# Moving the weight-splitting work of a fused delta-rule attention and MLP kernel ahead of its layer products

## The chip, the cores and the metric

The kernel runs on one core of one Trainium2 chip. A core has a matrix engine (TensorE, PE in the profile, with its weight loads shown as PEld), VectorE (DVE), ScalarE (ACT), GpSimd (POOL) and SyncE (SP), which here only issues DMAs. The metric is the device time of one execution in microseconds (us), lower is better; it is 635.78 us in the median of three runs (633.97 to 636.45).

## The reference

A delta-rule attention over 768 tokens for 4 batches of 8 heads of width 48, then a two-layer MLP with a squared relu on the 3072 tokens.

```python
# attention: q, k, v (4, 8, 768, 48), beta (4, 8, 768), all float32
k_n = k / (norm(k) + 1e-06)
for t in range(S):
    y[:, :, t] = einsum('bhd,bhde->bhe', q[:, :, t], state)
    v_old = einsum('bhde,bhd->bhe', state, k_n[:, :, t])
    state = state + beta_t * einsum('bhd,bhe->bhde', k_n[:, :, t], v[:, :, t] - v_old)
# MLP: x is y as (3072, 384); w_in (384, 2048), w_out (2048, 384)
h = maximum(x @ w_in, 0.0)
return (h * h @ w_out).astype(float32)
```

## The kernel before

**Units.** The 768 tokens are cut into 12 units of 64 tokens (u = 0 to 11). For each unit the kernel loads keys, queries, values and beta, normalizes the keys (`normalize`: squares on ACT, L310; their sums on DVE, L314; root, reciprocals, the scaling of the keys, L326), transposes keys and queries on PE and copies them out on ACT (L363, L366), forms the products of keys with keys and with queries (L379), inverts a triangular matrix for each head on DVE (`invert`, L556 and L557, for units 2 and on, and `invert_both` for units 0 and 1), carries the state on (`state_part`: L609, L620, L646, L671, L689, L706), and puts the unit's 256 rows (64 tokens of 4 batches) through the MLP (`moe`). The inversion of unit 2 works on a matrix `lt` that is written to DRAM in blocks and read back by DMA.

**The MLP of one unit.** `moe` transposes the rows, splits them into a high part x_h (ACT, L729) and a low part x_l (DVE, L730), and runs 8 pairs of layer steps. A first step is 9 products into a bank h (L762: high weights with x_h, low weights with x_h, high weights with x_l, 3 chunks each). When both steps of a pair are done, ACT does relu, square and a cast (L771, L772, L774) and DVE the low half h_l (L739). Two pairs later come the second-layer steps, 6 products each (L747), into two banks o. The 36 layer products of the title are the first four of these first-layer steps; a unit has 16 first-layer steps (9 products) and 16 second-layer steps (6 products).

**The weights.** w_in and w_out come from DRAM as 28 parts (numbered 0 to 27 in the order of loading, `w0` to `w27` in the names: 3 of w_in, 4 of w_out, and so on). Each is split on the chip into a high and a low half before it can be used, once: a scaling on ACT (L142), then **W** words (three DVE instructions, L150, L152, L154), **H** the cast to the high half on ACT (L160), **R** the remainder on DVE (L174), **L** the low half: two PE products into a PSUM bank (L167, L168) and a copy out of it on ACT (L169). The parts 0 to 9 are split before the first MLP; the parts 10 to 27 are split while unit 0's MLP runs, in two stretches: a hand-written order after `take(chain, 1)` (L895 to L926), and then the weave of u = 1, which lays the steps of several generators at places between 0 and 1. In the weave the low halves are not listed: `settle` (L227) is called after the products of a layer step of unit 0 and does one if there is a remainder more than there is a cast in hand, `word` does some if more than two parts are under way, and `half` does what is missing when a product needs it.

**Order.** Within each engine the instructions run in the order in which the program writes them (`tc.manual_schedule`); engines wait for each other by semaphores. So an instruction that waits holds up all that stand behind it on its engine. The low halves use one two-bank tile g in pairs (the first of a pair needs both copies, L169, of the pair before), and single banks x where `spare` is off. All loads of the stretch go through SP's queue in order: queries of unit 2 (L270, which wait until PE has transposed the queries of unit 1, L363), w20, w21, beta of unit 2, values of unit 1, then what the inversion of units 0 and 1 sends (L530, L535, after DVE's L519), w22 to w27, keys of unit 3, and the blocks for `lt` (L397, L407).

Of the kernel before, what the change touches and what calls it, by code (L numbers as in the profile page):

```python
# [21 lines left out]
def kernel(  # L22
# [96 lines left out]
    FIRST = 7  # L119
# [16 lines left out]
    def split_weights():  # L136
# [8 lines left out]
        def words(x):  # L145
            raw = raws[x]
            w1 = raw[:, :, 1]
            a, rest = room(x, w1.shape[1])

            nc.vector.tensor_scalar(out=a, in0=w1, scalar1=3, scalar2=None, op0=ALU.logical_shift_left)  # L150

            nc.vector.tensor_scalar(out=w1, in0=w1, scalar1=3, scalar2=-0x800000, op0=ALU.logical_shift_left,  # L152
                                    op1=ALU.bitwise_and)
            nc.vector.scalar_tensor_tensor(out=rest.bitcast(F32R), in0=raw[:, :, 0].bitcast(U32), scalar=2.0 ** -52,  # L154
                                           in1=w1.bitcast(F32), op0=ALU.mult, op1=ALU.mult)
            return x, a, rest
# [38 lines left out]
        def word():  # L195
            while woven[0] and summed and len(formed + casted + summed) > 2:
                join()
            formed.append(words(*ready.pop(0)))

        def cast():  # L200
# [6 lines left out]

        def join():
            low(*summed.pop(0), formed=True)

        steps_of = dict(W=word, H=cast, R=remain, L=join)

# [14 lines left out]
        def settle():  # L227

            if hold[0] or not woven[0]:
                hold[0] = max(0, hold[0] - 1)  # L230
            elif len(summed) > (len(casted) > 0):
                work("L")

        def half(*key):
# [1 line left out]
                work("L" if summed else "R")  # L236
            return halves[key]

        casted, summed = [], []
        ready, formed, waiting, done = [], [], [], [0]  # L240
        return scaled, worded, highs, lows, work, late(), settle, half

# [474 lines left out]
    def moe(d):  # L717
# [23 lines left out]
        def second(fp):  # L741
            h_h, h_l = hs[fp]
            for e in range(2):
                ft = 2 * fp + e
                for i in range(2):
                    for n, (a, w) in enumerate(((h_h, 0), (h_h, 1), (h_l, 0))):
                        nc.tensor.matmul(o[i], lhsT=a[:, e, i * P:(i + 1) * P], rhs=half("wo", ft)[w],  # L747
                                         start=(ft == 0 and n == 0), stop=(ft == FT - 1 and n == 2))
                if d["u"] == 0:
                    settle()  # L750
                rest()
                yield

        for fp in range(FT // 2):
            hp = ps_h.tile([P, PC], F32, name="h").rearrange("p (e t) -> p e t", e=2)
            for e in range(2):
                ft = 2 * fp + e
                f = slice(ft % EACH * P, (ft % EACH + 1) * P)
                n = 0
                for w, x in ((0, x_h), (1, x_h), (0, x_l)):  # L760
                    for kt in range(KT):
                        nc.tensor.matmul(hp[:, e], lhsT=half("wi", (kt, ft // EACH))[w][:, f], rhs=x[:, kt],  # L762
                                         start=(n == 0), stop=(n == 3 * KT - 1))
                        n += 1
                if e == 0:
                    if d["u"] == 0:
                        settle()
                    rest()
                    yield
            r = mpool.tile([P, 2, 2 * P], F32, name="r")  # L770
            nc.scalar.activation(out=r, in_=hp, func=AF.Relu)  # L771
            nc.scalar.activation(out=r, in_=r, func=AF.Square)  # L772
            h_h = mpool.tile([P, 2, 2 * P], F32R, name="h_h", bufs=3)
            nc.scalar.copy(out=h_h, in_=r)  # L774
            h_l = mpool.tile([P, 2, 2 * P], F32R, name="h_l", bufs=3)
            later.append((r, h_h, h_l))
            hs.append((h_h, h_l))
            yield
            if fp > 1:
                yield from second(fp - 2)  # L780
# [13 lines left out]
    def take(gen, n=None):  # L794
        while n is None or n > 0:
            try:
                next(gen)
            except StopIteration:
                return
            if n is not None:  # L800
                n -= 1
# [19 lines left out]
    def bank_spared():  # L821
        del halves_free[:]
        spare[0] = True
        yield

    def late_loads():
        load_beta(ds_[2])
        load_v(ds_[1])
        yield
        fetch(NW)  # L830
        yield
# [21 lines left out]
    with tc.manual_schedule(engines=engines):  # L853
# [53 lines left out]
        first, third = moe(ds_[0]), normalize(ds_[2])  # L907
        take(first, 1)
        split_early = False
        spare[0] = True  # L910
        work("L")
        take(first, 2)
        work("HRHR")
        take(first, 2)
        work("LL")
        take(chain, 1)
        take(pair[1], 2)
        work("WHRL")
        take(first, 1)
        take(pair[1], 1)  # L920
        load_q(ds_[2])
        fetch(2)
        take(third, 1)
        work("W")
        take(third, 1)
        work("HRL")  # L926
        spare[0] = False
        used = FIRST + 10
        before = None
        woven[0] = True  # L930
        corner, inverse = inverse, None
        for u in range(1, units):
            parts = []
            begun = J0 if u == 1 else I0
            n_i = round((1 - begun) / (I1 - begun) * NI)
            if inverse:
                parts.append((inverse, left))
            getting, now = loads(u), moe(ds_[u - 1]) if u > 1 else first
            parts += [(now, [-2])] if u > 1 else []
            if u < units - 1:  # L940
                parts.append((static(ds_[u + 1]), [-1, 0.155, 0.165] if u > 1 else [0.14, 0.215, 0.225]))
            inverse = invert(ds_[u + 1]) if u < units - 1 else None
            if inverse:
                parts.append((inverse, steps(n_i, begun, 1)))
                left = steps(NI - n_i, 0, I1 - 1) + [0.16]
            if u == 1:
                parts.append((corner, [0.01, 0.035, 0.075, 0.115, 0.12, 0.13]))
                parts.append((third, [0.01, 0.015, 0.03, 0.045]))
                parts.append((late_loads(), [0.08, 0.131]))
                parts.append((bank_spared(), [0.1305]))  # L950
                parts.append((splits, steps(2 * (NW - used) + 1, 0, 0.7)))
                parts.append((pair[1], [0.25]))
            parts += [(getting, L1 + steps(6, *N1) if u > 1 else [0.135] + steps(6, 0.55, 0.9)),
                      (state_part(ds_[u]), [x / STEPS for x in (CHAIN if u > 1 else CHAIN1)])]
            if before:
                parts += [(before, [x / STEPS for x in range(OVER)] + [0.2, 0.21])]
            parts.append((now, [x / STEPS for x in range(OVER, STEPS)] if u > 1 else steps(STEPS - OVER - 5, 0, 1)))
            weave(*parts)
            before = now
        final = moe(ds_[units - 1])  # L960
# [33 lines left out]
```

## Time and profile before

| what | value |
|---|---|
| median of 3 runs | 635.78 us (633.97 to 636.45) |
| the profiled execution | 635.26 us, span 633.5 us from the first to the last instruction |
| PE busy in the span | 591.6 us (93%) |
| DVE, ACT, POOL busy | 418.2 us (66%), 317.7 us (50%), 29.8 us (5%) |
| mean granted clock of TensorE | 0.96 of full speed |
| DMA | 49.32 MB, 78 GB/s on average |

Busy time is a sum over instructions of an engine. A matmul's end is modelled, so busy PE time is not work at the peak rate: at the lower of the two clocks (1.2 GHz instead of 2.4 GHz, shown as 0.50) the same products are busy for longer. Idle time of an engine that nothing waits for costs nothing.

### The profile page before, as it was taken

To read this page: it belongs to the slowest core of one execution; us is meant where nothing else is said; L and a number is where in the kernel's file an instruction comes from. 1 tells how busy PE (TensorE), PEld (TensorE's weight loads), DVE (VectorE), ACT (ScalarE), POOL (GpSimd) and SP (SyncE) were. 2 spreads that over 40 slices of the span, in tenths; PEclk is the share of its full clock that TensorE was granted. 3 is DMA by queue.
4 is the path that set the end of the run, shared out by engine and by line. 5 is a ranking of instruction groups with operands and counts; after the bars stand their busy time and mean duration, and the time that the engine had idled before them with its cause. 6 is when DMAs were issued, how large, how long until landed. Compare 5 with 4: busy or idle time off the path is not lost.

```text
span 633.5 us, 23879 instructions
## 1 busy us (share of the span) xinstructions
PE 591.6 (93%) x10390; PEld 557.8 (88%) x10390; DVE 418.2 (66%) x1130; ACT 317.7 (50%) x623; POOL 29.8 (5%) x52
## 2 busy tenths in 40 slices
PE   2859787899999999999999999999999999999997
PEld 2547676789999999999999999999999999999997
DVE  4697357798686694795794785875876865941211
ACT  4736655745454545445435536455454535355442
POOL 4000000000101001001001001001010010000000
PEclk9955779899999999999999999999999999999999
DMA  7667347612624524427217217226235144030101
GB/s 213 159 172 186 94 100 209 103 31 40 111 53 64 86 50 85 75 39 117 55 27 125 55 32 122 57 40 112 53 49 98 27 65 82 2 68 2 26 1 26
DMA packets 172464, 49.32 MB, mean 78 GB/s; under 512 B 164288, under 2 KB 167368, under 8 KB 172360
## 3 DMA queue, kind: packets, MB, share of 16 engines
q1 hardware_dynamic: 168840, 47.06, 37.1%
q8 instruction: 82, 1.34, 0.9%
q10 hardware_dynamic: 3392, 0.72, 0.6%
q14 instruction: 22, 0.18, 0.1%
q0 software_dynamic: 128, 0.01, 0.0%
HBM read 36.54 MB, written 10.49 MB: 74 GB/s over the span
## 4 chain that ended last, share of the span: by engine, by line
PE 80%; ACT 2%; issue 0%; DVE 0%; ACTq 0%; DVEq 0%
PE o L747 32%; PE h L762 31%; PE g L646 2%; PE x L646 2%; PE x L671 2%; PE g L706 2%; PE x L379 1%; PE g L379 1%; PE x L689 1%; PE h L609 1%; PE x L620 1%; PE h L726 1%; PE x L363 1%; PE g L363 1%; ACT w L169 0%
## 5 line engine op out<-in xcount | busy, mean ns | idle before, releaser
L747 PE MATMUL o<-w,h_h 128*128 128x384 f32 x768 | 204.7, 348 | 0.0
L771 ACT ACTIVATE r<-h 128x512 f32<-128x512 f32 x96 | 57.5, 599 | 231.9 <-PE h L762 231.8
L762 PE MATMUL h<-x_h,w 128*128 128x256 f32 x1152 | 171.9, 285 | 0.4 <-DVE x_l L730 0.3
L739 DVE TENSOR_TENSOR h_l<-r,h_h 128x512 fp32r<-128x512 f32 x96 | 67.7, 705 | 139.3 <-ACT h_h L774 139.3
L762 PEld LDWEIGHTS h<-x_h,w 128*128 128x128 f32 x1152 | 156.4, 192 | 2.0 <-ACT x_h L729 0.8
L747 PEld LDWEIGHTS o<-w,h_h 128*128 128x128 f32 x768 | 134.5, 189 | 3.2
L747 PE MATMUL o<-w,h_l 128*128 128x384 f32 x384 | 130.4, 340 | 0.0
L556 DVE SCALAR_TENSOR_TENSOR tmp<-lt,bt,z 128x126 f32<-128x126 f32 (+22 forms) x310 | 95.7, 309 | 9.5 <-DMA lt<-blocks 1.7
L762 PE MATMUL h<-x_l,w 128*128 128x256 f32 x576 | 100.7, 284 | 0.0
L557 DVE TENSOR_TENSOR z<-z,tmp 128x126 f32<-128x126 f32 (+22 forms) x310 | 79.2, 256 | 10.6
L762 PEld LDWEIGHTS h<-x_l,w 128*128 128x128 f32 x576 | 82.8, 191 | 0.0
L747 PEld LDWEIGHTS o<-w,h_l 128*128 128x128 f32 x384 | 72.6, 189 | 0.0
L772 ACT ACTIVATE r<-r 128x512 f32<-128x512 f32 x96 | 60.7, 632 | 3.1
L774 ACT CAST h_h<-r 128x512 fp32r<-128x512 f32 x96 | 59.5, 620 | 3.1
L545 POOL MEMSET z<- 128x512 f32 x10 | 5.3, 527 | 454.8 <-DMA inv<-z 273.4
L697 DVE TENSOR_TENSOR state<-state,x 48x384 f32<-48x384 f32 x40 | 22.0, 550 | 0.8 <-PE x L689 0.3
L379 PE MATMUL x<-kq 48*64 48x64 f32 (+1 forms) x608 | 19.1, 255 | 0.7 <-ACT kq L366 0.7
L379 PEld LDWEIGHTS x<-kq 48*64 48x64 f32 x608 | 16.8, 152 | 2.8 <-ACT kq L366 1.1
L142 ACT ACTIVATE w<-w 128x384 f32<-128x384 f32 (+1 forms) x28 | 16.7, 613 | 4.6 <-DMA w<-in_moe_w_in_dram 4.6
L363 PE MATMUL x<-plus,kpad 64*128 64x64 f32 x96 | 6.5, 240 | 11.3 <-DVE kpad L326 11.3
L624 ACT ACTIVATE tt<-x 32x256 f32<-32x256 f32 x44 | 16.4, 373 | 0.5
L154 DVE SCALAR_TENSOR_TENSOR rest<-w 128x384 fp32r<-128x384 uint32 (+1 forms) x21 | 13.3, 634 | 4.5 <-PE g L168 2.4
(150 smaller groups left out, 627.9 us busy)
## 6 DMA issues: line engine op xcount, KB each, us to landing
w<-in_moe_w_in_dram SPq DMA_DIRECT2D x12, 512.0 KB
w<-in_moe_w_out_dram SPq DMA_DIRECT2D x16, 384.0 KB
lt<-blocks SPq DMA_DIRECT2D x20, 256.0 KB
qpad<-in_q_dram SPq DMA_DIRECT2D x96, 48.0 KB
vt<-in_v_dram SPq DMA_DIRECT2D x48, 96.0 KB
out_dram<-a SPq DMA_DIRECT2D x46, 96.0 KB
kpad<-in_k_dram SPq DMA_DIRECT2D x88, 48.0 KB
blocks<-ap SPq DMA_DIRECT2D x40, 64.0 KB
```

Of the source, the lines that this page charges most:

```text
L363: nc.tensor.transpose(pair[b][:, x, p], src[rows, c, 2 * p:2 * p + 2].rearrange("p a b -> p (a b)"), ident[rows, rows])
L379: nc.tensor.matmul(ps[j][to * C:(to + 1) * C, p, (x - first) * C:(x - first + m) * C], lhsT=kq[rows, c, p, b, 0], rhs=kq[rows, c, p, b, x: ...
L556: nc.vector.scalar_tensor_tensor(out=tmp, scalar=bt[:, s:s + 1], op0=ALU.mult, op1=ALU.mult, **factors)
L557: nc.vector.tensor_tensor(out=z[:, :nj, s + 1:], in0=z[:, :nj, s + 1:], in1=tmp, op=ALU.subtract)
L646: nc.tensor.matmul(dst[j][to, c, p], lhsT=d["kq"][rows, c, p, b, x], rhs=state[rows, b, c, p], start=(c == 0 and p == 0) if x else True, s ...
L697: nc.vector.tensor_tensor(out=state[rows, b], in0=state[rows, b], in1=ku[b][rows], op=ALU.add)
L739: nc.vector.tensor_tensor(out=h_l, in0=r, in1=h_h.bitcast(F32), op=ALU.subtract)
L747: nc.tensor.matmul(o[i], lhsT=a[:, e, i * P:(i + 1) * P], rhs=half("wo", ft)[w], start=(ft == 0 and n == 0), stop=(ft == FT - 1 and n == 2))
L762: nc.tensor.matmul(hp[:, e], lhsT=half("wi", (kt, ft // EACH))[w][:, f], rhs=x[:, kt], start=(n == 0), stop=(n == 3 * KT - 1))
L771: nc.scalar.activation(out=r, in_=hp, func=AF.Relu)
L772: nc.scalar.activation(out=r, in_=r, func=AF.Square)
L774: nc.scalar.copy(out=h_h, in_=r)
```

## The change

Unit 0's MLP and the splitting of parts 11 to 27 are written in another order. In the hand-written stretch the low halves and casts stand ahead of the first layer steps, and the squares of the third keys (unit 2) directly after the first relu. In `moe`, `settle` is called ahead of a layer step's products, where before it was called behind them, and it is called for the second step of a pair (in the first layer from the fourth pair on for both). `settle` has another condition (a counter `ripe`: a remainder that was made before the last `word`). In the weave of u = 1 the places of the inversion of units 0 and 1 (`corner`), of unit 2's transposes and of the late loads are moved back by 0.02 to 0.04, and the MLP has one step fewer left.

```diff
@@ split_weights
         def word():
             while woven[0] and summed and len(formed + casted + summed) > 2:
                 join()
+            ripe[0] = len(summed)
             formed.append(words(*ready.pop(0)))
 ...
         def join():
             low(*summed.pop(0), formed=True)
+            ripe[0] = max(0, ripe[0] - 1)
 ...
             if hold[0] or not woven[0]:
                 hold[0] = max(0, hold[0] - 1)
-            elif len(summed) > (len(casted) > 0):
+            elif ripe[0] or summed and not formed and not ready:
                 work("L")
@@ moe, second layer
                 ft = 2 * fp + e
+                if d["u"] == 0 and e:
+                    settle()
                 for i in range(2):
                     for n, (a, w) in enumerate(((h_h, 0), (h_h, 1), (h_l, 0))):
 ...
-                if d["u"] == 0:
-                    settle()
                 rest()
@@ moe, first layer
                 ft = 2 * fp + e
+                if d["u"] == 0 and (e or fp > 2):
+                    settle()
                 f = slice(ft % EACH * P, (ft % EACH + 1) * P)
 ...
                 if e == 0:
-                    if d["u"] == 0:
-                        settle()
                     rest()
@@ the hand-written stretch
-        spare[0] = True
-        work("L")
+        spare[0] = woven[0] = True
+        hold[0] = 0
+        work("LHRHRL")
         take(first, 2)
-        work("HRHR")
+        take(third, 1)
         take(first, 2)
-        work("LL")
+        take(third, 1)
         take(chain, 1)
+        work("W")
+        take(first, 1)
         take(pair[1], 2)
-        work("WHRL")
+        work("HR")
+        take(third, 1)
         take(first, 1)
         take(pair[1], 1)
         load_q(ds_[2])
         fetch(2)
-        take(third, 1)
-        work("W")
-        take(third, 1)
-        work("HRL")
         spare[0] = False
-        used = FIRST + 10
+        used = FIRST + 9
         before = None
-        woven[0] = True
@@ the weave of u = 1
-                parts.append((static(ds_[u + 1]), [-1, 0.155, 0.165] if u > 1 else [0.14, 0.215, 0.225]))
+                parts.append((static(ds_[u + 1]), [-1, 0.155, 0.165] if u > 1 else [0.18, 0.25, 0.26]))
 ...
-                parts.append((corner, [0.01, 0.035, 0.075, 0.115, 0.12, 0.13]))
-                parts.append((third, [0.01, 0.015, 0.03, 0.045]))
-                parts.append((late_loads(), [0.08, 0.131]))
+                parts.append((corner, [0.03, 0.075, 0.12, 0.16, 0.165, 0.17]))
+                parts.append((third, [0.005, 0.02, 0.03]))
+                parts.append((late_loads(), [0.08, 0.171]))
```

No instruction is added or removed on any engine; on POOL nothing moves, and SP's DMAs keep their order.

The first place is ACT, from the first relu of unit 0's MLP on (`h_960` and `h_971` are the first pair's bank, `kpad2` the third keys, `g_954` the bank with the low halves of parts 10 and 11). Before:

```order
L771 ACTIVATE r_979<-h_960 128x512
L772 ACTIVATE r_979<-r_979 128x512
L774 CAST h_h_982<-r_979 128x512
L160 CAST w13_985<-r_886 128x384
L142 ACTIVATE w15_705<-w15_705 128x512
L142 ACTIVATE w16_707<-w16_707 128x512
L160 CAST w14_990<-a_892 128x512
L771 ACTIVATE r_1013<-h_993 128x512
L772 ACTIVATE r_1013<-r_1013 128x512
L774 CAST h_h_1016<-r_1013 128x512
L169 CAST w11_833<-g_954 128x384
L169 CAST w12_883<-g_1022 128x384
```

And in the changed program, whose lines from the relu on are two higher:

```order
L160 CAST w13_958<-r_886 128x384
L142 ACTIVATE w15_705<-w15_705 128x512
L142 ACTIVATE w16_707<-w16_707 128x512
L160 CAST w14_963<-a_892 128x512
L169 CAST w11_833<-g_954 128x384
L773 ACTIVATE r_990<-h_971 128x512
L774 ACTIVATE r_990<-r_990 128x512
L776 CAST h_h_993<-r_990 128x512
L312 ACTIVATE kq_999<-kpad2_104 128x384 x2
L773 ACTIVATE r_1022<-h_1002 128x512
L774 ACTIVATE r_1022<-r_1022 128x512
L776 CAST h_h_1025<-r_1022 128x512
```

The weights' work has moved ahead of the first relu, and the third keys' squares stand between the first relu and the second; in both programs the copies of the new state (L693 before, L695 now) come next.

The second place is DVE where the first step of unit 2's inversion (128x31, the first reader of `lt`) stands. Before:

```order
L174 TENSOR_TENSOR w24_1716<-a_1705,w24_1716 128x384
L654 TENSOR_TENSOR vt_1330<-vt_1330,x_1743 128x8x48
L654 TENSOR_TENSOR vt_1330<-vt_1330,x_1744 128x8x48
L150 TENSOR_SCALAR a_1797<-w26_1400 128x384
L152 TENSOR_SCALAR w26_1400<-w26_1400 128x384
L154 SCALAR_TENSOR_TENSOR rest_1798<-w26_1400 128x384
L556 SCALAR_TENSOR_TENSOR tmp_1810<-lt_1555,bt_1324,z_1802 128x31
L557 TENSOR_TENSOR z_1802<-z_1802,tmp_1810 128x31
L739 TENSOR_TENSOR h_l_1793<-r_1788,h_h_1791 128x512
L556 SCALAR_TENSOR_TENSOR tmp_1810<-lt_1555,bt_1324,z_1802 128x30
L557 TENSOR_TENSOR z_1802<-z_1802,tmp_1810 128x30
L174 TENSOR_TENSOR w25_1739<-a_1734,w25_1739 128x384
```

And in the changed program:

```order
L656 TENSOR_TENSOR vt_1291<-vt_1291,x_1757 128x8x48
L656 TENSOR_TENSOR vt_1291<-vt_1291,x_1758 128x8x48
L174 TENSOR_TENSOR w24_1730<-a_1711,w24_1730 128x384
L741 TENSOR_TENSOR h_l_1756<-r_1751,h_h_1754 128x512
L558 SCALAR_TENSOR_TENSOR tmp_1812<-lt_1569,bt_1285,z_1804 128x31
L559 TENSOR_TENSOR z_1804<-z_1804,tmp_1812 128x31
L150 TENSOR_SCALAR a_1815<-w26_1425 128x384
L152 TENSOR_SCALAR w26_1425<-w26_1425 128x384
L154 SCALAR_TENSOR_TENSOR rest_1816<-w26_1425 128x384
L558 SCALAR_TENSOR_TENSOR tmp_1812<-lt_1569,bt_1285,z_1804 128x30
L559 TENSOR_TENSOR z_1804<-z_1804,tmp_1812 128x30
L174 TENSOR_TENSOR w25_1793<-a_1734,w25_1793 128x384
```

The words of part 26 have moved behind the first reader of `lt`, and a low half h_l ahead of it; the remainder of part 25 stands behind it in both.

The third place is PE at the low halves of parts 24 and 25 (`plus_87` is the identity with which a low half is summed). Before:

```order
L167 MATMUL g_1872<-w24_1716,plus_87 128x384
L168 MATMUL g_1872<-rest_1706,plus_87 128x384
L747 MATMUL o0_958<-w13_985,h_h_1484 128x384 x2
L747 MATMUL o0_958<-w13_985,h_l_1486 128x384
L747 MATMUL o1_959<-w13_985,h_h_1484 128x384 x2
L747 MATMUL o1_959<-w13_985,h_l_1486 128x384
L762 MATMUL h_1898<-x_h_934,w21_1604 128x256
L762 MATMUL h_1898<-x_h_934,w22_1626 128x256
L762 MATMUL h_1898<-x_h_934,w23_1654 128x256
```

And in the changed program:

```order
L167 MATMUL g_1872<-w24_1730,plus_87 128x384
L168 MATMUL g_1872<-rest_1712,plus_87 128x384
L751 MATMUL o0_969<-w13_958,h_h_1371 128x384 x2
L751 MATMUL o0_969<-w13_958,h_l_1373 128x384
L751 MATMUL o1_970<-w13_958,h_h_1371 128x384 x2
L751 MATMUL o1_970<-w13_958,h_l_1373 128x384
L167 MATMUL g_1872<-w25_1793,plus_87 128x384
L168 MATMUL g_1872<-rest_1735,plus_87 128x384
L766 MATMUL h_1896<-x_h_934,w21_1614 128x256
L766 MATMUL h_1896<-x_h_934,w22_1641 128x256
L766 MATMUL h_1896<-x_h_934,w23_1707 128x256
```

The low half of part 25, which stood behind the first layer step on `h_1898`, now stands ahead of it.

## Rows read from the trace of the kernel before

**Rows 1.** Windows: stretch, its length, busy time (count) of each engine, granted clock, DMA.
```profile
70.90:81.40 10.50, 9.15 (x157) 7.84 (x157) 1.76 (x4) 5.06 (x13) 0.00 (x0) 0.53 0.20 35
81.40:84.40 3.00, 1.44 (x66) 0.99 (x66) 2.53 (x7) 2.36 (x6) 0.00 (x0) 0.96 0.58 151
84.40:90.60 6.20, 6.20 (x87) 5.36 (x81) 4.72 (x13) 3.01 (x6) 0.00 (x0) 0.50 0.37 113
90.60:114.30 23.70, 18.12 (x393) 15.56 (x392) 17.76 (x33) 14.87 (x29) 1.96 (x3) 0.99 0.65 164
114.30:118.50 4.20, 4.20 (x27) 3.87 (x17) 1.88 (x4) 1.41 (x4) 0.00 (x0) 0.59 0.18 32
137.10:633.50 496.40, 491.68 (x8397) 474.76 (x8394) 324.63 (x903) 237.60 (x453) 19.48 (x27) 1.00 0.34 60
```

**Rows 2.** Timeline, 64 to 76 us: start, duration, engine, line; in brackets idle before.
```profile
64.70 0.60 ACT L771 ACTIVATE r<-h 128x512 f32<-128x512 f32 x1 [3.42 <-PE h L762]
66.00 0.62 ACT L774 CAST h_h<-r 128x512 fp32r<-128x512 f32 x1
70.39 0.47 ACT L169 CAST w<-g 128x384 fp32r<-128x384 f32 x1
70.91 0.69 PE L167 MATMUL g<-w,plus 128*128 128x384 f32 x1 [3.83 <-ACT w L169]
73.86 0.86 ACT L693 COPY state<-x 128x384 f32<-128x384 f32 x2 [1.42 <-PE x L689]
74.39 1.50 PE L363 MATMUL x<-plus,qpad 64*128 64x64 f32 x16 [0.58 <-ACT state L693]
75.39 5.33 SPq L270 DMA_DIRECT2D qpad<-in_q_dram  x8
```

**Rows 3.** Timeline from 87 us: SP's queue, and what waits for its loads.
```profile
87.64 3.12 SPq L264 DMA_DIRECT2D vt<-in_v_dram  x4
93.97 0.42 DVE L519 TENSOR_TENSOR lt<-lt,g 128x256 f32<-128x256 f32 x1 [2.14 <-PE g L517]
94.47 2.63 SPq L530 DMA_DIRECT2D t1t<-lt  x4
100.60 1.10 SPq L128 DMA_DIRECT2D w<-in_moe_w_in_dram  x2
104.82 0.68 ACT L142 ACTIVATE w<-w 128x512 f32<-128x512 f32 x1 [4.57 <-DMA w<-in_moe_w_in_dram]
122.08 0.24 DVE L556 SCALAR_TENSOR_TENSOR tmp<-lt,bt,z 128x31 f32<-128x31 f32 x1
146.87 1.02 DVE L730 TENSOR_TENSOR x_l<-h,x_h 128x384 fp32r<-128x384 f32 x2
```

**Rows 4.** Timeline: lengths of single pieces of work.
```profile
75.83 1.07 ACT L366 COPY kq<-x 128x512 f32<-128x512 f32 x2 [1.11 <-PE x L363]
79.84 0.65 ACT L426 COPY ap<-x 128x256 f32<-128x256 f32 x2 [1.61 <-PE x L379]
81.26 0.95 ACT L310 ACTIVATE kq<-kpad 128x384 f32<-128x384 f32 x2
83.69 0.80 PE L507 MATMUL g<-lt,ap 32*32 32x16 f32 x64 [1.53 <-ACT w L169]
92.63 0.39 PE L167 MATMUL x<-w,plus 128*128 128x512 f32 x1
93.19 0.73 PE L517 MATMUL g<-t1t,z 16*32 16x16 f32 x64
```

**Rows 5.** Chain that ended last, in order of time: start, length, what.
```profile
162.44 1.08 PE x L646 x64
201.61 2.12 PE o L747 x12
203.72 2.14 PE h L762 x18
```

**Rows 6.** Windows of one microsecond (columns as in rows 1).
```profile
69.00:70.00 1.00, 0.00 (x0) 0.00 (x0) 0.90 (x3) 0.94 (x3) 0.00 (x0) 1.00 0.01 3
```

More of the change, by code (lines that the diff above doesn't have):

```diff
@@ L237, in half @@
             return halves[key]
-        casted, summed = [], []
+        casted, summed, ripe = [], [], [0]
         ready, formed, waiting, done = [], [], [], [0]
@@ L946 @@
             if u == 1:
-                parts.append((corner, [0.01, 0.035, 0.075, 0.115, 0.12, 0.13]))
-                parts.append((third, [0.01, 0.015, 0.03, 0.045]))
-                parts.append((late_loads(), [0.08, 0.131]))
-                parts.append((bank_spared(), [0.1305]))
+                parts.append((corner, [0.03, 0.075, 0.12, 0.16, 0.165, 0.17]))
+                parts.append((third, [0.005, 0.02, 0.03]))
+                parts.append((late_loads(), [0.08, 0.171]))
+                parts.append((bank_spared(), [0.1705]))
                 parts.append((splits, steps(2 * (NW - used) + 1, 0, 0.7)))
-                parts.append((pair[1], [0.25]))
-            parts += [(getting, L1 + steps(6, *N1) if u > 1 else [0.135] + steps(6, 0.55, 0.9)),
+                parts.append((pair[1], [0.2]))
+            parts += [(getting, L1 + steps(6, *N1) if u > 1 else [0.175] + steps(6, 0.55, 0.9)),
                       (state_part(ds_[u]), [x / STEPS for x in (CHAIN if u > 1 else CHAIN1)])]
@@ L956 @@
                 parts += [(before, [x / STEPS for x in range(OVER)] + [0.2, 0.21])]
-            parts.append((now, [x / STEPS for x in range(OVER, STEPS)] if u > 1 else steps(STEPS - OVER - 5, 0, 1)))
+            parts.append((now, [x / STEPS for x in range(OVER, STEPS)] if u > 1 else steps(STEPS - OVER - 6, 0, 1)))
             weave(*parts)
```

## The prediction

> **What bounds the kernel now.** I read three views: the windows, the timeline with its waits, and the chain that ended last. From 137.1 us to the end PE is busy for 491.7 of 496.4 us at full clock [rows 1]: that part is bound by PE, the change leaves its order alone, and what the change gains or loses is the time at which PE comes there. Ahead of it, while unit 0's MLP runs and the weights are split, PE both waits and runs slowly. The granted clock is 0.53 over the 10.5 us from 70.9, 0.50 over the 6.2 us from 84.4, 0.59 over the 4.2 us from 114.3, so mostly at the lower level, 1.2 GHz [rows 1]. In the same rows PE idles for 1.3, 1.6, 0, 5.6 and 0 us, and it waited 3.8 us just before them [rows 2]. The reader should see which wait ends last. The 3.8 us are PE at part 12's low half, waiting for ACT's copy of part 11's at 70.39, which stands behind two relu groups [rows 2]. Then runs one long chain: ACT copies the state at 73.86, PE transposes the queries, and only that lets SP go on at 75.39 [rows 2]. SP issues until 90.8 (87.64 + 3.12), waits for DVE's L519 (done at 94.4), sends the inverse from 94.47, loads part 22 from 100.60 [rows 3]. ACT has stood 4.6 us for that load when it starts at 104.82. The blocks of `lt` follow in the same queue, DVE starts unit 2's inversion on them at 122.08, and 24.8 us later it makes x_l of unit 1, which PE needs [rows 3]. So SP's queue, `lt` and DVE pace this stretch more than PE's own work does.
>
> **The change, step by step.** I use durations at full clock: 9 products of a first-layer step take 1.07 us and 6 of the second layer 1.06 (halves of 2.14 and 2.12), a group of 64 small state products 1.08 [rows 5].
>
> *1. Earlier state copy.* Part 11's low half now stands ahead of the first products. It is two products, the first 0.69 at the low clock [rows 2]; as x_l would be waited for anyway and the clock rises soon, I take 0.4 us of delay (between 0 and 1.4, twice 0.69). The first relu starts at 64.7 + 0.4 = 65.1. A relu group takes 1.92 (64.70 to 66.62 [rows 2]), so it ends at 67.0; the squares (0.95 [rows 4]) at 68.0, the second relu group at 69.9. The state products no longer wait for part 12's low half, so the copy starts at 69.9 instead of 73.86, 4.0 sooner. The transposes took 1.50 at the low clock and SP started 1.53 behind the copy [rows 2]; at full clock I take 0.2 off (0 to 0.4). SP goes on 4.2 us sooner, at 71.2.
>
> *2. SP no longer waits for L519.* From its start to the end of the values SP needs 90.76 - 75.39 = 15.4 us, so it is ready for the inverse at 86.6. Is L519 done by then? State copy 0.86 and transposes about 0.7 from 69.9: 71.5. Query copies 1.07: 72.6. Four short ACT instructions, estimated 1.6 from L169's 0.47 each: 74.2. A relu group 1.92 and four copies of 0.33: 77.4. Then PE: two L507 groups of 0.80, three low halves of 0.56 (92.63 to 93.19), two second-layer and two first-layer steps, two L517 groups of 0.73 [rows 4, 5]: 1.6 + 1.7 + 4.3 + 1.5 = 9.1, less the last low half and last step, which overlap waits or stand behind it, up to 1.2. So 85.3 to 86.5, with L519's 0.42 [rows 3] 85.7 to 86.9. About level: the 3.7 us between 90.76 and 94.47 go, less 0 to 0.3. I take 3.7. L530 starts at 86.6, 7.9 us sooner.
>
> *3. What hangs on SP.* Its issues behind that keep their order, so part 22's scaling moves from 104.82 to about 96.9 and the first step of unit 2's inversion from 122.08 to 114.2. On DVE part 26's words stand behind it instead of ahead, one h_l and part 24's remainder ahead instead of behind: about even. x_l of unit 1 would come 7.9 sooner.
>
> *4. The waits PE gets instead.* Low halves now stand ahead of layer steps, so a late one holds up products that would have run. Part 20's needs the copies of parts 18 and 19, which stand on ACT behind part 22's scaling: 96.9 + 2.7 = 99.6, while PE is there at about 96.5: 3.1 us. Part 22's stands behind one h_l and part 23's words on DVE: about 2.5 us. Part 25's needs a remainder behind the first reader of `lt`: two inversion steps, part 26's words, the remainder, 2.8 us together, so 117.0, while PE is there at 113.2: 3.8 us. With smaller ones PE waits some 15 us by this ledger, no less than before. What pays is that the stretches at low clock behind 70.9 and 84.4 mostly fall into full clock: 9.15 and 6.20 us of busy time [rows 1] were worth about half of that.
>
> *5. The end.* From 117.0 PE has three low halves of 0.5, six layer steps and state work, 11.2 us together, plus 1.8 of waits (part 25's copy, part 26's remainder): state done at 130.0. It was done at 137.1 with one more first-layer step to do: 7.1 + 1.07 = 8.2 us. But behind the 3.8 us wait I expect the low clock, as at 70.91 [rows 2]. It lasted 4.2 and 6.2 us in the dense stretches [rows 1], which costs half, 2.1 to 3.1, of which the 1.8 us of waits swallow most: 1.2 (0 to 3.4). The sum is 8.2 - 1.2 = 7.0, below the 7.9 that DVE allows.
>
> Behind the wait of 3.8 us the granted clock was 0.53 for 10.5 us [rows 1, 2]. The Trainium skill, TensorE: Matmul & The Clock Gate, in HAM oscillation — how this bites in real kernels, has the rule: a long enough wait throttles PE, and each batch of matmuls behind such a wait starts at the low rate again. That speaks against a change that gathers PE's idle time into three longer waits; by the rule all three are paid for and the time is rival B's, 631.0, by the forecast one of them and 628.8. The trace agrees for its longest wait and does not settle it for the shorter ones.
>
> **The sum.** The profiled execution took 635.26; less 7.0 gives 628.3. It lies 0.5 below the median of the runs, so for the median 628.8.
>
> **The rivals.** *A: the clock falls already in the gaps before the L507 group.* By my ledger PE waits 2.1 of the 4 us ahead of that group (0.7 for part 13's copy, 1.4 for the relu group and the four copies); between 81.4 and 84.4 it worked 1.44 of 3.00 us, and then the clock was 0.50 [rows 1]. Then the products up to L519 run at 1.2 GHz for 4.2 to 6.2 us and L519 ends 2.1 to 3.1 later; SP waits some 2, and 5.0 is left: 630.8. Against it: from 90.6 to 114.3 the clock stayed at 0.99 with 5.6 us idle [rows 1].
>
> *B: low clock after each long wait, and long after the last.* If it lasts 10.5 us as from 70.9 [rows 1], step 5 costs 5.2 less 1.8, 3.4 instead of 1.2: 4.8 left, 631.0; with A too 2.8, 633.0, no measurable change.
>
> *C: slower, by the clock.* From 77 to 130 PE has 39 us of full-clock work and 13 of waits. If every gap keeps it at 1.2 GHz, that takes 78 us instead of 53: 25 - 8.2 = 17 us slower, 653. It decides from the point where the cost passes 8.2 + 3.2, that is over 23 us at low clock even if no wait swallowed any; before there were 20.9 us [rows 1]. Against it: long dense stretches from 77 to 96, and the clock rose in each such stretch before.
>
> *D: the third keys are late.* Their squares now stand ahead of the second relu, so ACT's whole queue waits if they haven't landed at 67.0. No load was on its way at 69 to 70 (DMA share 0.01 [rows 6]), so that is at most 2.0 us: 5.0 left, 630.8.
>
> **How the numbers follow.** Chances: forecast 0.48, A or D 0.25, B alone 0.08, A with B or another cause that leaves under 3.2 us 0.13, C 0.06. A measurement of this kernel tells about 0.5% (3.2 us) from no change: faster 0.81, same 0.13, slower 0.06. The range: at the fast end no cost of the low clock (8.2 left, 627.6) step 1's favourable ends (0.6) and half a microsecond for the estimated pieces, 626.5; at the slow end A with B, 633.0. It leaves out C and half of the fourth case.
>
> **What would show it.** Step 1: the state copy on ACT near 70, SP's query loads near 71, no 3.8 us wait at part 12. Step 2: no wait of SP on L519; L530 near 87. Step 3: part 22's scaling near 97, the 31-wide inversion step near 114. Step 4: PE waits of 2.5 to 4 us at parts 20, 22 and 25. Step 5: full clock at 77 to 96, a low stretch from about 117, state done near 131. I am wrong if squares or relu hold ACT past 71, if the clock between 72 and 90 is near 0.5, or if DVE reaches the first reader of `lt` later than the data.

## The result and the profile after

The changed kernel takes 627.17 us (median of 4 runs, 626.52 to 630.92) against 635.40 of the kernel before in the same series: a ratio of 0.988, 95% interval 0.984 to 0.993. The forecast was 628.8, in a range of 626.5 to 633.0. A second series gave 627.80 against 635.32 (0.9895, 0.987 to 0.992). The profiled execution has a span of 624.8 us (633.5 before).

The windows of the kernel after, over the stretches that [rows 1] shows of before, with the one ahead of them. The columns behind the length are busy time and instructions of PE, PEld, DVE, ACT and POOL, then the granted clock, the DMA share and GB/s.

```profile
60.00:70.90 10.90, 8.90 (x131) 8.31 (x132) 5.58 (x11) 8.44 (x17) 0.00 (x0) 1.00 0.55 143
70.90:81.40 10.50, 9.22 (x292) 7.95 (x290) 8.00 (x20) 8.38 (x20) 0.00 (x0) 1.00 0.51 125
81.40:84.40 3.00, 3.00 (x103) 2.73 (x92) 1.21 (x4) 2.54 (x5) 0.43 (x1) 1.00 0.08 20
84.40:90.60 6.20, 5.41 (x132) 4.70 (x128) 5.96 (x10) 4.50 (x10) 1.53 (x3) 1.00 0.50 89
90.60:114.30 23.70, 17.83 (x269) 15.56 (x267) 16.09 (x35) 13.38 (x27) 0.00 (x0) 0.86 0.84 193
114.30:118.50 4.20, 1.43 (x11) 1.33 (x11) 3.92 (x13) 3.01 (x8) 0.00 (x0) 1.00 0.37 64
...
128.50:624.80 496.30, 490.86 (x8385) 473.85 (x8385) 324.28 (x902) 237.47 (x453) 19.28 (x27) 1.00 0.34 60
```

The three stretches that were at 0.53, 0.50 and 0.59 [rows 1] are at full clock; a low one has come up between 90.6 and 114.3. The dense part is as it was: 491 of 496 us, only it begins at 128.5 instead of 137.1.

The timeline of the kernel after, the rows that answer to [rows 2, 3] (start, length, engine, line, operation; in brackets the idle time ahead and what ended it). Lines behind the relu stand two lower in the file than before: L693, L519 and L530 are now L695, L521 and L532.

```profile
66.72 0.52 ACT L312 ACTIVATE kq<-kpad 128x384 f32<-128x384 f32 x1 [1.48 <-DMA kpad<-in_k_dram]
...
68.94 0.85 ACT L695 COPY state<-x 128x384 f32<-128x384 f32 x2
...
70.29 6.29 SPq L272 DMA_DIRECT2D qpad<-in_q_dram  x8
...
83.94 0.42 DVE L521 TENSOR_TENSOR lt<-lt,g 128x256 f32<-128x256 f32 x1 [1.79 <-PE g L519]
86.39 3.01 SPq L532 DMA_DIRECT2D t1t<-lt  x4
...
96.58 0.65 ACT L142 ACTIVATE w<-w 128x512 f32<-128x512 f32 x1 [5.92 <-DMA w<-in_moe_w_in_dram]
97.14 0.46 ACT L169 CAST w<-g 128x384 fp32r<-128x384 f32 x1
...
97.65 0.69 PE L167 MATMUL g<-w,plus 128*128 128x384 f32 x1 [4.54 <-ACT w L169]
...
110.90 1.02 DVE L656 TENSOR_TENSOR vt<-vt,x 128x384 f32<-128x384 f32 x2 [1.50 <-PE x L648]
...
112.91 0.25 DVE L558 SCALAR_TENSOR_TENSOR tmp<-lt,bt,z 128x31 f32<-128x31 f32 x1
...
116.64 0.48 ACT L169 CAST w<-g 128x384 fp32r<-128x384 f32 x1
...
117.17 0.44 PE L167 MATMUL g<-w,plus 128*128 128x384 f32 x1 [2.77 <-DVE w L152]
...
138.18 1.02 DVE L732 TENSOR_TENSOR x_l<-h,x_h 128x384 fp32r<-128x384 f32 x2
```

Each station of the chain is sooner: the state copy by 4.9 us, SP's queries by 5.1, the inverse by 8.1, part 22's scaling by 8.2, the first inversion step by 9.2, x_l by 8.7. SP no longer waits for DVE. The 3.83 us that PE stood at part 12 [rows 2] are gone; it now stands 4.54 us at part 19's low half and 2.77 us at part 25's. Both waits end with a copy on ACT (97.14 + 0.46 and 116.64 + 0.48, each 0.05 us ahead of the product), although the row puts the second down to DVE's L152. DVE comes to the first inversion step (112.91) without idle time ahead of it, as it did before at 122.08 [rows 3]: it did not stand waiting for `lt` in either kernel. Its last wait ahead of that step is for PE's L648, at 110.90.

### The profile page after: what moved, and what is told of

It is laid out like the page before. It is cut to its first block, busy times and chain, and to the rows that moved or that the text cites. A ratio compares the mean times of both kernels' runs of the same rounds, so it can differ in the third digit from the quotient of the medians.

```text
span 624.8 us, 23884 instructions
## 1 busy us (share of the span) xinstructions
PE 583.0 (93%) x10390; PEld 550.8 (88%) x10390; DVE 417.9 (67%) x1130; ACT 317.1 (51%) x623; POOL 29.5 (5%) x52
## 4 chain that ended last, share of the span: by engine, by line
PE 80%; DVE 1%; DMA 0%; ACT 0%; issue 0%
PE o L751 32%; PE h L766 31%; PE g L648 2%; PE x L648 2%; PE x L673 2%; PE g L708 2%; PE x L381 1%; PE g L381 1%; PE x L691 1%; PE x L622 1%; PE h L611 1%; PE h L728 1%; PE x L365 1%; PE g L365 1%; DMA kpad<-in_k_dram 0%
## 5 line engine op out<-in xcount | busy, mean ns | idle before, releaser
L766 PE MATMUL h<-x_h,w 128*128 128x256 f32 x1152 | 169.2, 283 | 0.1
L766 PEld LDWEIGHTS h<-x_h,w 128*128 128x128 f32 x1152 | 154.8, 189 | 1.3 <-issue 0.3
L699 DVE TENSOR_TENSOR state<-state,x 48x384 f32<-48x384 f32 x40 | 22.0, 550 | 0.8 <-PE x L691 0.3
L550 POOL TENSOR_SCALAR_AFFINE_SELECT z<-z 64x512 f32<-64x512 f32 x20 | 16.0, 799 | 1.4
```

Source lines behind the costliest of these rows:

```text
L699: nc.vector.tensor_tensor(out=state[rows, b], in0=state[rows, b], in1=ku[b][rows], op=ALU.add)
```

## The experiments

Every kernel here ends 495.7 to 497.6 us behind the moment at which DVE starts adding the new state (L697, L699): 633.5 - 137.04 before, 624.8 - 128.36 after. So most of what differs lies ahead of that moment, and from the state copy to it each trace gives a ledger in one row of the windows: its length is PE's idle time (length less busy time), what the low clock costs (busy time times one minus the granted clock; roughly, since the mean clock counts idle time as well), and the rest, PE's work at full speed. The rows of before, of after, and of three of the experiments:

```profile
73.86:137.04 63.18, 53.02 (x1092) 46.02 (x1092) 43.52 (x108) 37.83 (x80) 1.96 (x3) 0.86 0.47 109
```
```profile
68.94:128.36 59.42, 48.03 (x1092) 42.33 (x1092) 45.69 (x113) 37.46 (x80) 1.96 (x3) 0.94 0.52 119
```
```profile
71.02:137.67 66.65, 54.83 (x1079) 49.48 (x1080) 45.99 (x113) 37.36 (x80) 1.96 (x3) 0.82 0.46 103
```
```profile
71.07:130.20 59.13, 51.09 (x1084) 45.17 (x1085) 45.92 (x112) 37.25 (x80) 1.96 (x3) 0.88 0.52 116
```
```profile
70.67:125.68 55.01, 50.98 (x1121) 43.42 (x1119) 45.89 (x112) 37.29 (x80) 1.96 (x3) 1.00 0.58 125
```

They are, in this order, before, after, old places, keys behind and filled waits. The same for all, in us, with the time of each against the kernel before on the same chip:

| kernel | state copy | length | PE idle | low clock costs | median | ratio (95%) |
|---|---|---|---|---|---|---|
| before | 73.86 | 63.18 | 10.2 | 7.4 | 635.40 | 1 |
| after | 68.94 | 59.42 | 11.4 | 2.9 | 627.17 | 0.988 (0.984 to 0.993) |
| after, again | 69.91 | 59.28 | 10.8 | 2.9 | 627.80 | 0.990 (0.987 to 0.992) |
| stretch alone | 68.97 | 61.20 | 11.3 | 5.5 | 628.82 | 0.991 (0.989 to 0.994) |
| old places | 71.02 | 66.65 | 11.8 | 9.9 | 633.94 | 0.998 (0.996 to 1.001) |
| low halves behind | 69.98 | 61.62 | 11.7 | 5.5 | 631.25 | 0.993 (0.992 to 0.995) |
| old stretch | 73.57 | 66.60 | 11.1 | 11.7 | 637.37 | 1.004 (1.002 to 1.005) |
| longer queue | 70.76 | 66.23 | 15.4 | 5.1 | 635.56 | 1.001 (0.999 to 1.002) |
| weights sooner | 70.97 | 59.50 | 10.3 | 4.4 | 629.14 | 0.990 (0.988 to 0.993) |
| beta elsewhere | 69.41 | 59.35 | 9.5 | 4.5 | 627.80 | 0.989 (0.987 to 0.991) |
| later inverse | 71.35 | 61.65 | 10.2 | 4.1 | 629.56 | 0.991 (0.989 to 0.994) |
| keys behind | 71.07 | 59.13 | 8.0 | 6.1 | 628.65 | 0.991 (0.988 to 0.993) |
| keys and beta | 72.00 | 58.88 | 7.8 | 6.1 | 627.38 | 0.989 (0.986 to 0.992) |
| filled waits | 70.67 | 55.01 | 4.0 | 0.0 | 623.79 | 0.983 (0.982 to 0.985) |

What is left of the length, the work at full speed, is 43.9 to 45.7 us in all but two rows (47.4 with the later inverse, which has 13 PE instructions more in the stretch than after; 51.0 with filled waits, 4.4 of it the fillers). So idle time and low clock account for most of the differences in length. The 3.83 us wait of before [rows 2] lies ahead of its state copy and so outside its row. The ledger is of one execution each, and that execution lies between 1.5 us below the median of its kernel (low halves behind) and 2.9 above it (later inverse). The state copy itself moves by some 3 us between kernels that are the same up to there (68.94 to 72.00): the clock of the stretch ahead of it differs from execution to execution (from 60 us to the copy it was 1.00 in the kernel after and 0.72 in its second profile). Profiles are therefore best compared by the length, and times by the medians.

### Which part of the change does it

**Old places**: the change, with its places in the weave taken back.

```
-parts.append((static(ds_[u + 1]), ... [0.18, 0.25, 0.26]))
+parts.append((static(ds_[u + 1]), ... [0.14, 0.215, 0.225]))
-parts.append((corner, [0.03, 0.075, 0.12, 0.16, 0.165, 0.17]))
+parts.append((corner, [0.01, 0.035, 0.075, 0.115, 0.12, 0.13]))
```
(and late_loads, bank_spared, pair[1] and the loads in the same way)

> The changed kernel with the old places of the weave of u = 1 (inversion of units 0 and 1, unit 2's transposes, late loads), everything else as changed. Theory Q (SP's queue, started by unit 1's query transposes, paces the stretch by way of lt): the places are no part of the gain, since L519 was done 2 us before SP was ready for it; 626 to 629 us, SP's L530 at 86 to 87. Rival W (the places in the weave pay): 630 us or more.

633.94 us: the places matter, as the rival had it. But not by the queue: SP sent the inverse at 88.68, only 0.5 us behind its readiness. The granted clock over the length was 0.82, and 7.0 of the 7.2 us by which the stretch is longer than in the kernel after are low clock.

**Low halves behind**: the change, with the calls of settle behind the layer steps and its old condition.

```
-elif ripe[0] or summed and not formed and not ready:
+elif len(summed) > (len(casted) > 0):
 ... (and the calls of settle, moved back)
```

> The changed kernel with settle called behind the layer steps again and with its old condition; the hand-written stretch and the weave's places stay changed. Theory Q: the state copy stays near 69 and SP's query loads near 70, so most of the gain stays: 627 to 630 us. Rival S (low halves ahead of the layer steps are what pays, by shorter waits of PE): 633 to 636 us.

631.25 us, between the two and nearer to Q: the new order of the low halves is worth some 4 us where the places are new (3.5 to 4.1 by the medians; the intervals just touch).

**Old stretch**: the change, with the hand-written stretch of before (state copy and squares as there).

> The changed kernel with the hand-written stretch of before (low halves and squares late), but settle and the weave's places as changed. Theory Q: the state copy is back near 73 to 74 and SP's query loads near 75, so at least the 4 to 5 us of that step are lost: 631 to 636 us. Rival S (settle's place pays): 626 to 629 us.

637.37 us. The state copy is back at 73.57 and SP's inverse at 94.15, and the gain is gone; the time lies a little above what Q gave.

**Stretch alone**: the kernel before, with nothing but the new stretch.

> The kernel before with only the hand-written stretch of the change (casts, remainders and two low halves ahead of the first products, the third keys' squares sooner): places of the weave and of the low halves as before. Theory Q (the state copy's lead is passed on through SP's queue): the state copy comes at 70 to 71 instead of 73.6, SP's queries at 72, so at least 2.5 us of the lead is there, and the wait for L521 stays, since the old places keep L521 at 88 or later as in the run with old places (634): 633 to 635, and half or more of the change's gain is missing. The other theory, that the earlier state copy alone is the gain (4 us and more, whatever stands behind it): 628 to 631.

628.82 us, so Q fell here, and the time lies where the other theory had it: the stretch alone has 6 of the 7 to 8 us, with SP's wait for L519 down from 3.7 to 1.5 us, and the rest of the change adds 1.0 to 1.7 us to it, too little to be told apart. Of the six, some 4.1 are the earlier state copy (9.4 us behind x_l of unit 0 instead of 13.5) and 2.0 the shorter length; that the low halves, the casts and the squares of the stretch have a part of their own in this was not tested one by one. Put together: new low halves without new places cost 5.1 us on top of the stretch (633.94 - 628.82), new places without new low halves 2.4 (631.25 - 628.82, with intervals that overlap), both together gain a little. For the 5.1 the ledger says why: the same idle time of 11.3 to 11.8 us in all three, but a low clock that costs 5.5 in the stretch alone, 9.9 with the new low halves in the old places, and 2.9 with both. The 2.4 it does not explain: the low clock costs 5.5 there as well, and the length is only 0.4 longer.

### Is it SP's queue that sets the end?

**Longer queue**: eight extra copies from DRAM to DRAM behind unit 2's queries in SP's queue.

```
+for n in range(8):
+    nc.sync.dma_start(out=dram.tile([C, 4, D], F32, name=f"idle{n}", bufs=1), in_=tokens(q, ds_[2])[0][:, 0, ::2])
```

> The changed kernel with eight more DMA issues of a key load's shape in SP's queue behind unit 2's queries (about 0.6 us each, 4.9 us together, DRAM to DRAM, nobody reads them). Theory Q: everything behind them comes 4.9 us later and the end too, 631 to 632.5 us; the first step of unit 2's inversion moves from 112.9 to 117 to 118. Rival C (PE's work at full clock paces the stretch, the queue is slack): 626.5 to 628.5 us.

The timeline of this kernel, SP's queue:

```profile
77.90 6.23 SPq L929 DMA_DIRECT2D idle<-in_q_dram  x8
...
94.54 3.10 SPq L532 DMA_DIRECT2D t1t<-lt  x4
```

635.56 us: 6.23 us of issues cost about 8, all of the gain. Counted from the state copy the inverse goes 6.3 us later. Idle time rose by 4.0 and low clock by 2.2. Whatever hangs on SP there is on the path, as step 3 had it, but by way of part 22: ACT stood 8.45 us for its load (5.92 in the kernel after), while DVE came to the first inversion step, at 121.55, without a wait for `lt`. Whether the extra copies' own traffic has a part in it was not tested. Does a shorter queue gain?

**Weights sooner**: parts 22 and 23 are fetched ahead of the inverse.

```
 load_v(ds_[1])
+fetch(2)
 yield
```

> The loads of parts 22 and 23 stand in SP's queue behind the values and ahead of the inverse instead of behind it (two issues of 0.55 us move ahead of the eight of L532 and L537, 5.6 us, which stand 1.1 us later). Theory P (PE's waits are what counts now): in the changed kernel ACT stood 5.92 us for part 22 and PE 4.54 us at part 19's low half behind it, and low clock followed to 101.5; the load lands 5.6 us sooner, so that wait falls under 1 us. The inverse lands 1.1 later, the blocks of lt keep their place, and the next thing that is late is the first 31-wide inversion step, which cannot come before 111.5. So the gain stops near 1.5 to 3 us: 624 to 626. Theory Q (the path through SP to lt sets the end): nothing on that path is sooner and the inverse is 1.1 us later, so 627 to 628.5.

629.14 us. ACT's wait for part 22 fell from 5.92 to 0.29 us and PE's at part 19 went, but DVE now waited for `lt` and PE at part 25. The timeline of this kernel:

```profile
113.29 0.25 DVE L558 SCALAR_TENSOR_TENSOR tmp<-lt,bt,z 128x31 f32<-128x31 f32 x1 [2.33 <-DMA lt<-blocks]
...
117.55 0.69 PE L167 MATMUL g<-w,plus 128*128 128x384 f32 x1 [5.19 <-DVE w L152]
```

The idle time moved from one low half to another; theory P fell, and the time lies a little above what Q gave too.

**Beta elsewhere**: unit 2's beta is issued from POOL's queue.

```
-queue = nc.gpsimd if d["u"] == 0 else nc.sync
+queue = nc.gpsimd if d["u"] in (0, 2) else nc.sync
```

> Unit 2's beta (four issues of 2.76 us in sum, a wait of 1.6 and a copy of 0.57 on SP) is issued from POOL's queue. SP would be ready for the inverse 5 us sooner, at 81.4, but waits for L521, done at 84.4, so that the inverse, part 22's load and the blocks all move 1.9 us sooner. Theory Q: 625 to 625.5. Theory P: the wait for part 22 falls by 1.9 us as well, and if the clock does not fall behind what is left of it (2.6 us) another 1 to 1.9 us come back: 623.5 to 625. A rival, that the copy of beta was no cost since its queue is not what anything waits for: 627.

627.80 us, no gain, and not because nothing waits for that queue: counted from the state copy, the inverse went 2.0 us sooner (15.4 instead of 17.4 behind it), PE's wait at part 19 fell to 3.06 us and part 25's low half came 1.5 us sooner (46.7 instead of 48.2 behind it). What came behind it took that back. The timeline of this kernel:

```profile
116.13 0.44 PE L167 MATMUL g<-w,plus 128*128 128x384 f32 x1 [2.77 <-DVE w L152]
116.41 0.46 PE L168 MATMUL g<-rest,plus 128*128 128x384 f32 x1
116.66 1.49 PE L766 MATMUL h<-x_h,w 128*128 128x256 f32 x6
```

The same six products in the kernel after, and the windows around this low half, first of the kernel after, then of beta elsewhere:

```profile
117.62 0.87 PE L766 MATMUL h<-x_h,w 128*128 128x256 f32 x6
```
```profile
114.00:120.00 6.00, 3.23 (x79) 2.68 (x77) 5.62 (x19) 3.49 (x9) 0.00 (x0) 1.00 0.32 56
```
```profile
114.00:120.00 6.00, 3.87 (x63) 3.65 (x67) 5.61 (x18) 3.13 (x9) 0.00 (x0) 0.72 0.31 54
```

The six products take 1.49 us; in the kernel after they took 0.87 behind a wait of the same 2.77 us, and the granted clock from 114 to 120 us was 1.00 there and 0.72 here. From this low half to the finished state it took 12.6 us instead of 11.2.

**Later inverse**: J0, where unit 2's inversion begins, 0.62 instead of 0.56.

> Unit 2's inversion begins at 0.62 of the weave instead of 0.56: on DVE part 26's words and the remainders of parts 25 and 26 stand ahead of the first inversion steps instead of among them. Theory P: part 26's cast on ACT, its four copies of L626 and the copy of part 24's low half come some 0.6 us sooner, so that the 2.77 us wait of PE at part 25 falls to about 2.1 and the time by 0.5 to 0.8: 626 to 626.7. Theory Q in its strict form (the end follows the first reader of lt): that reader comes 1.2 us or more later and the time rises by as much: 628 to 629.

629.56 us, on the side of Q: part 25's wait fell only to 2.38, and low clock followed it all the same.

**Keys behind**: weights sooner, and unit 3's keys between the blocks' way out and the read of `lt` (the loads' place 0.255 instead of 0.175). **Keys and beta**: with beta elsewhere too.

> As the run with weights sooner, and unit 3's keys (eight issues, 6 to 8 us of SP) stand between the blocks' way out and the read of lt instead of ahead of both, so that lt is read some 2.8 us sooner (in that run SP stood 1.7 us between 105.75 and 107.47 for the blocks, and the keys now fill that). Theory of two paths that end together (the wait for part 22 and the path through SP to lt; taking away one only moves PE's wait to the other): with both shortened the 31-wide inversion step no longer waits for a DMA and comes at some 40 us behind the state copy instead of 42.3, PE's wait at part 25 falls from 5.2 to about 2.8 us, the state is done some 57 us behind its copy instead of 59.4, and the time is 625 to 626.5. Theory that PE's clock or DVE's own work sets the distance of 59.4 us: it stays, and the time is 627.5 to 629.

> As the run with keys behind, and unit 2's beta issued from POOL's queue, so that the values, part 22's load and the inverse move up to 1.9 us sooner on SP. Theory of two paths: both are shorter by 1 to 2 us again, but DVE itself is ready for the inversion step only 39.9 us behind the state copy, so that little is left to gain: 624.5 to 626.5, level with or up to 1 us below the run with keys behind. Theory that the distance of 59.4 us stays: 627.5 to 628.5.

628.65 and 627.38 us. Both paths are shorter, unit 2's inversion does not wait for `lt` as it did with weights sooner, PE's idle time is 3.4 and 3.6 us below that of the kernel after, and the length is nearly what it was there: the low clock costs 6.1 instead of 2.9. The theory of two paths fell. The timeline of keys behind shows a place where the clock fell:

```profile
99.19 0.75 PE L611 MATMUL h<-tt,ap 32*32 32x32 f32 x64
101.78 0.80 PE L167 MATMUL g<-w,plus 128*128 128x512 f32 x1 [1.83 <-ACT w L169]
102.37 0.63 PE L168 MATMUL g<-rest,plus 128*128 128x512 f32 x1
102.80 0.84 PE L751 MATMUL o<-w,h_h 128*128 128x384 f32 x2
```

Two second-layer products take 0.84 us there and 0.51 at full clock.

### Is it the clock?

**Filled waits**: keys and beta, and PE multiplies by zeros in its two longest waits (9 and 14 products, added to an accumulator that stays what it was; `plus[:C, C:]` is a corner of zeros).

```
 ... (o and x_h of unit 0's MLP are handed in)
+for _ in range({21: 9, 25: 14}.get(x, 0)):
+    nc.tensor.matmul(o[0][:C], lhsT=plus[:C, C:], rhs=x_h[:C].rearrange("p k t -> p (k t)")[:, :DM],
+                     start=False, stop=False, skip_group_check=True)
 ps = split_bank()[:, :hl.shape[2]]
```

> As the run with keys behind and beta on POOL's queue, and PE works in its two longest waits: 9 extra products of 64 rows of zeros (384 columns, some 0.17 us each at full clock) ahead of part 21's low half, 14 ahead of part 25's. They add zero to an accumulator and need nothing that is late. In that run PE idled 7.8 us between the state copy and the finished state, which is 3.6 less than in the changed kernel, but low clock took the gain back: 6.0 us of its busy time by the granted clock, against 2.2. Theory that the clock falls in those waits and is what holds the time: the granted clock stays near 1.00 from 98 to 120, the loss falls from 6.0 to 2 or less, the state is done 55 to 57 us behind its copy instead of 58.9, then x_l on DVE is the next thing that PE waits for, and the time is 623.5 to 625.5. Theory that the two paths through DVE, ACT and SP set the distance whatever the clock does: 627 to 628.5. If the extra products cost time themselves: 629 or more.

The timeline of this kernel (L166 are the fillers):

```profile
99.33 1.79 PE L166 MATMUL o<-x_h,plus 64*64 64x384 f32 x9
101.25 0.50 PE L171 MATMUL g<-w,plus 128*128 128x512 f32 x1
...
111.67 2.65 PE L166 MATMUL o<-x_h,plus 64*64 64x384 f32 x14
114.51 0.44 PE L171 MATMUL g<-w,plus 128*128 128x384 f32 x1 [0.19 <-ACT w L173]
```

623.79 us (623.55 to 624.83), 3.6 less than without the fillers, and the fastest of all kernels here. The clock is 1.00 from the state copy to the finished state, the length 55.0. x_l, which was to be waited for next, was not: it came sooner as well, at 135.51. The fillers held nothing up: both low halves start 0.05 us behind ACT's copy (done at 101.20 and 114.46), as they do without fillers. The five runs also lie closer together, within 1.3 us instead of the 4.4 and 4.9 of the kernel after. So the clock is what held the time in keys and beta. The fillers on the changed kernel alone, without the shorter queue, were not tried.

## Why the prediction was right, step by step

**Step 1, the earlier state copy**: said 4.0 us sooner at 69.9, SP's queries at 71.2. The profile has 68.94 and 70.29, that of the second series 69.91 and 71.25; counted from x_l of unit 0 ahead of it the copy comes 9.7 and 10.4 us later instead of 13.5, so the change gives 3.1 to 3.8, and the rest of the 4.9 lies ahead of that x_l, where the clock differs from execution to execution. The new stretch, in which this step stands, carries the gain: the run with the stretch alone has 6 of the 7 to 8 us, some 4 of them in the copy, the run without it none.

**Step 2, SP no longer waits for L519**: right, the inverse at 86.4 and 86.9 against 86.6. The stretch alone leaves 1.5 us of the 3.7, so most of this step too comes from the stretch and not from the places.

**Step 3**: part 22's scaling at 96.6 and 97.4 (said 96.9), the first inversion step at 112.9 and 113.8 (114.2), x_l at 138.2 and 139.0 (139.0). The times fit, but the path to the inversion step is another than the one described: it was not `lt` that came last there, in either kernel, but DVE, whose row has no idle time ahead. So the prediction's sign of being wrong, that DVE reaches the first reader later than the data, did occur. DVE had waited for PE's L648 (1.50 us), which stands behind the wait at part 19, and that hangs on part 22's load: SP's queue sets the time by way of the weights. The two paths lie close, since with weights sooner DVE did wait 2.33 us for `lt`.

**Step 4, the new waits**: this is where the working was wrong most. The long wait is at part 19, not at part 20, the 2.5 us at part 22 did not come, and part 25's was 2.8 instead of 3.8. The step took a low half to wait for the copies of the two before it; in the program's waits the second low half of a two-bank tile also waits for ACT's copy of the first, so part 19 waits for part 18's, which stood behind part 22's scaling, and part 25 for part 24's. Its sum was too high, some 15 us, where PE idles 11.4 from the state copy on. What held is that from the copy on the gain is not idle time, of which there were 10.2 us before, but low clock that went, 7.4 us to 2.9.

**Step 5**: the low clock that was expected behind part 25's wait (1.2 us) came behind part 19's instead, from 97.65 to about 102.4, where it costs half of 4.75 us, 2.4. The end of it in the timeline of the kernel after, where L167 is back from the 0.69 us of 97.65 to 0.42:

```profile
101.98 0.52 PE L751 MATMUL o<-w,h_l 128*128 128x384 f32 x1
102.30 0.42 PE L167 MATMUL g<-w,plus 128*128 128x384 f32 x1
```

The state is done at 128.4 and 129.2 (said 130.0); the gain is 7.5 to 8.2 by medians for 7.0. That the end fits so well while the waits and the low clock stand at other parts, with other lengths, is in part luck.

**Rivals.** A (low clock ahead of L507's group) did not occur: 1.00 from 70.9 to 90.6. B did not either, but more narrowly than the 0.08 given to it says: behind the same wait of 2.77 us the clock stayed at 1.00 in both profiles of the changed kernel and fell with beta elsewhere. The Trainium skill's rule that the prediction weighed (TensorE: Matmul & The Clock Gate, HAM oscillation — how this bites in real kernels) fits the 4.54 us wait; the 2.77 us wait of the changed kernel is one behind which the batch did not start at the low rate. That all three of its waits were long enough for the rule was the prediction's own reading. C did not occur in the kernel after, but old places, where the low clock costs 9.9 us, shows that a change of this kind can lose its gain to the clock. D occurred in one of the two profiles and was hidden: the third keys held the second square for 1.48 us, but the first relu came at 62.9 instead of 65.1. In the other profile the relu came at 65.45 and the keys were there.

What the prediction did not see is that its own gain hung on two parts of the change fitting each other: next to the stretch alone, the new low halves without the new places give 5 us back, and the new places without the new low halves some 2, which is not clear of the spread.

## What to carry to other kernels

Split a stretch with many short waits into work, idle time and low clock before a wait is priced: here 3.6 us of waits were taken away and came back, to within 0.5 us, as low clock. Where PE has to stand, harmless products in the wait cost nothing here and kept the clock, which was worth 3.6 us. And when one copy releases a whole queue, put it ahead of the work that merely fills its engine: the stretch that does so had six of the change's seven to eight microseconds, some four of them in that copy.

## What the runs showed of the hardware

The length of a wait did not tell whether the clock falls. Behind 2.77 and 2.78 us the granted clock stayed at 1.00 in three profiles (the changed kernel twice, longer queue), and behind 2.74 to 2.82 it fell in four others (beta elsewhere, old places, keys behind, keys and beta); with a wait of 1.83 us it fell as well (keys behind). Even 1.49 us did both: in the old stretch the clock was 0.53 over the 3 us behind it, from 100.70, and in the stretch alone 1.00, from 94.71. What decides between them is open. Products with a 64-row corner of zeros as weights held the clock as real ones do: 1.00 over 55 us, with 4.0 us idle.
